# Attention, two MLPs: the second MLP wholly through a seven-product form, the second half of the attention moved beside the first MLP

## Chip, cores and metric

One core of one Trainium2 chip runs the whole program in one launch. The metric is the device time of that core in microseconds (us). Engines: PE multiplies matrices (PEld is its weight load), DVE, ACT and POOL do elementwise work, SP issues nearly all the DMAs.

## Reference

All arrays are float32 at the interface. `q`, `k`, `v` are 8 batches x 8 heads x 576 tokens x 64, `p` has 32 packed queries per head.

```python
def sm_attn(qq, kk, vv):
    s = scale * np.matmul(qq, kk.transpose(0, 1, 3, 2))
    s = s - np.max(s, axis=-1, keepdims=True)
    a = np.exp(s)
    a = a / (np.sum(a, axis=-1, keepdims=True) + 1e-09)
    return np.matmul(a, vv)
p_packed = sm_attn(p, k, v)
out = sm_attn(q, p_packed, p_packed)
...
x = out.transpose(0, 2, 1, 3).reshape(4608, 512)
xn = x / rms * rms_g
g = xn @ w_gate                                  # 512 x 1536
x = (g * (1.0 / (1.0 + np.exp(-g))) * (xn @ w_val)) @ w_out
h = x @ w_in                                     # second MLP, 512 x 2048
g = np.maximum(0.01 * h, h)
return g @ w_out                                 # 2048 x 512
```

The weights come as float64; the kernel turns them into float32 on the chip.

## The kernel before, in words

**Precision.** A value that matters is split into a high and a low part (ACT copies it to a reduced form, DVE or POOL subtracts: `split`, `sub`, L160 to L166), and `mm3` (L135) multiplies with three products: high by high, low by high, high by low. Some products run instead on plain float32 operands; the trace shows each of those as two matrix instructions.

**Attention.** A unit is one batch and four heads, so 16 units. `soft1` (L252) makes the packed keys and values of a unit, `soft2` (L419) the second attention and the sums of squares. Each of their operations has a place in tables (`ONE`, `TWO`), counted in slots; `slot()` (L1009) runs what is due. From unit `FAST` on, the scores are three products of split parts; from unit `FASTQ` on, the squares (`xp`) are. `atf`, which holds a batch's normalised attention, has one buffer.

**First MLP.** Batches go in four pairs; a pair is 24 steps, so 96 steps (L1309). A step multiplies 288 tokens by 256 columns of gate and value weights (24 products of 288 columns: tiles `g`, `v`), and adds the output of the step before to `y_acc` (24 products more: `y`). Four slots pass in a step. In each four steps `fold` (L875) multiplies the attention's packed values into the weights twice (tile `pwps`).

**Second MLP, z stage.** Between the first MLP's step 47 and step 48, tokens 0 to 2047 go through the second MLP in 64 rounds (L1353): 12 products of 512 columns into `zh` (`stage3z`), 12 into `zo` (`stage4z`). Beside them run units 8 to 15 of the attention (`NA = 8`; `LATER`: 22 slots a unit) and half of the 32 conversions of the second MLP's weights (`split_w2`). The other half stands in steps 24 to 39.

**Second MLP, seven products.** At the end tokens 2048 to 4607 go in three pairs of halves (`HALF`, widths 448, 448, 384). A pair needs seven products of sums and differences of the blocks (`ORDER`) where eight plain ones would be needed: 7 x 8 x 6 matrix products into `h` and as many into `o`. Their weights come as pieces of 256 KB through a ring of 10 buffers (`RING = (9, 1)`: 9 in pool `bw0`, which can be filled before the first MLP ends, 1 in pool `bw`). `sums_work` (L1206) makes the sums and differences of weights beside the steps from 48 on.

**Order.** The code is handed to a scheduler, which fixes every engine's instruction order before the run; an engine takes its instructions in that order. SP's queue is one such order: a DMA that waits holds up those behind it.

Of the kernel before, what the change touches and what calls it, by code (L numbers as in the profile page):

```python
# [40 lines left out]
)  # L41
SPLITW = (-68, -58, -57, -57, -8, -6, -1, -1, 9, 10, 13, 13, 21, 29, 29, 29, 37, 37, 45, 42, 50, 53, 59, 61,)
# [4 lines left out]
LATER = (0, 22)  # L47
ZEND = 51
WBUFS = 8
FAST = 8  # L50
FASTQ = 6
# [5 lines left out]
RING = (9, 1)  # L57
GBUFS = 9
CUT = 3
YS0 = 4  # L60
SUM0 = 0
EVERY = (1, 4)
# [4 lines left out]
def pack_attention_moe_kernel(  # L67
# [52 lines left out]
    at_dram = dram.tile([B, P, 2, S], F32, name="at_dram")  # L120
    op_dram = dram.tile([4, 4, P, DM], F32, name="op_dram")
# [3 lines left out]
    cvt = tc.alloc_tile_pool(name="cvt", bufs=1, side="right", reuse_waits="tile")  # L125
    mlpa = tc.alloc_tile_pool(name="mlpa", bufs=1, side="right", reuse_waits="tile")
    mlpb = tc.alloc_tile_pool(name="mlpb", bufs=1, side="right", reuse_waits="tile")
    mlpc = tc.alloc_tile_pool(name="mlpc", bufs=1, side="right", reuse_waits="tile")
    keep = tc.alloc_tile_pool(name="keep", bufs=1, side="left", reuse_waits="tile")
# [54 lines left out]
    g_sb = const.tile([P, KT], F32, name="g_sb")  # L184

# [64 lines left out]
    NA = 8  # L250

    def soft1(i):  # L252
# [4 lines left out]
        def keys():  # L257
# [10 lines left out]
            if i + 1 < NU and i + 1 != NA:  # L268
                last = load_k(*divmod(i + 1, 2))
# [88 lines left out]
        def packed():  # L358
# [21 lines left out]
            if i + 1 < NU and i + 1 != NA:  # L380
                load_v(*divmod(i + 1, 2))
# [33 lines left out]
        if i < NA:  # L415
            return list(zip(ONE[i], parts))
        return [(LATER[0] + LATER[1] * (i - NA) + at, f_) for at, f_ in zip(S1, parts)]

    def soft2(i):  # L419
# [14 lines left out]
        def queries(cs):  # L434
# [6 lines left out]
            if cs[-1] == 1:  # L441
                raw.pop(("q", b, u))
                if i >= FAST:
                    st["qh"] = att.tile([P, NS, 2, T], F32R, tag="raw", bufs=raws, name="qh" + nm)
                    st["ql"] = att.tile([P, NS, 2, T], F32R, tag="tr", bufs=2, name="ql" + nm)
                    split(qT, st["qh"], st["ql"])
                if i + 1 < NU and i + 1 != NA:
                    load_q(*divmod(i + 1, 2))
# [162 lines left out]
        def final(cs, x):  # L611
# [10 lines left out]
            if len(halves) == 2 and 2 * b >= NA:  # L622
                nc.sync.dma_start(out=at_dram[b], in_=atf.pop(b))
# [7 lines left out]
        late = LATER[0] + LATER[1] * (i - NA + 1)  # L631
        for at, f_ in zip(TWO[i] if i < NA else [late + at for at in S2], ops):
            out.append((at, lambda f_=f_: f_(cs)))
# [22 lines left out]
    def load_at(b):  # L656
        if NA <= 2 * b < NU:
            atf[b] = keep.tile([P, 2, S], F32, tag="atf", bufs=1, name=f"atr{b}")
            nc.sync.dma_start(out=atf[b], in_=at_dram[b])

    def split_at(b, cs=(0, 1)):
# [7 lines left out]
        assert 2 * b >= NA or {("at", b, 0), ("at", b, 1)} <= made  # L669
# [4 lines left out]
        if NA <= 2 * b:  # L674
            load_at(b + 1)
# [9 lines left out]
    def convert(raw64, hl, name, whole=False, lay=None):  # L685
# [5 lines left out]
        def begin():  # L691
            c = st["c"] = (
                hl if whole else cvt.tile([P, n], F32, tag="conv", bufs=2, name="cv" + name)
# [25 lines left out]
        def tail():  # L719
# [116 lines left out]
    NW2A = 16  # L836

    def w2_src(i):
        f4, k4 = i // 8, i % 4
        if i % 8 < 4:  # L840
            return w2_in[k4 * P : k4 * P + P, f4 * 512 : f4 * 512 + 512], w1_dram[f4, :, k4]
        m = 4 * f4 + k4
        return w2_out[m * P : m * P + P, :], w2_dram[f4, :, k4]
# [15 lines left out]
    def split_w2(i):  # L859
        if i < 32:  # L860
            until(lambda: i in w2q)
            t = cvt.tile([P, 1024], F32R, tag="w2", bufs=2, name=f"w2s{i}")
            convert(w2q.pop(i), t, f"w2{i}", lay=by_unit if i % 8 < 4 else by_block)

            def done():
                flush_store()
                stores.append((w2_src(i)[1], t))
                if i + 1 != NW2A:
                    load_w2(i + 1)
# [126 lines left out]
    for si in range(4 * NFG - 8, len(steps)):  # L996
        n1, kt = si // 4 + 1, si % 4
        if kt % 2:
            if n1 >= NFG:
                folds[si] = ((n1, kt // 2),)  # L1000
            splits[si] = (n1 * KT + KT + kt - 1, n1 * KT + KT + kt)
# [15 lines left out]
    w1, w2 = {}, {}  # L1017
    ys = {}


    trickle = []

    def drop(count=1, pin=False):
        for _ in range(min(count, len(trickle))):
            ins = trickle.pop(0)()
            if pin:
                tc.keep_in_program_order(ins)

    def load_part(t, src, k_):
        ks = slice(2 * k_, 2 * k_ + 2)  # L1030
        return nc.sync.dma_start(out=t[:, ks].bitcast(F32), in_=src[:, ks])

    def load_w1sb(pool, f, tag=None):
        tags = dict(tag=tag, bufs=1) if tag else {}
        t = w1[f] = pool.tile([P, 4, 1024], F32R, name=f"w1{f}", **tags)
        trickle.extend(lambda k_=k_: load_part(t, w1_dram[f], k_) for k_ in range(2))

    def load_w2sb(pool, f, tag=None):
        tags = dict(tag=tag, bufs=1) if tag else {}
        t = w2[f] = pool.tile([P, 4, 1024], F32R, name=f"w2{f}", **tags)  # L1040
        trickle.extend(lambda k_=k_: load_part(t, w2_dram[f], k_) for k_ in range(2))

    out_st = out.rearrange("(b t s) d -> b s t d", b=B, t=T)

    def store_rows(n, ob, es):

        at, end = n * (P // T), (n + 1) * (P // T)
        while at < end:
            b, s0 = divmod(at, NS)
            k_ = min(end - at, NS - s0)  # L1050
            p0 = (at - n * (P // T)) * T
            nc.sync.dma_start(
                out=out_st[b, s0 : s0 + k_, :, es],
                in_=ob[p0 : p0 + k_ * T, es],
            )
            at += k_


    NZ = 4
    yz = {}  # L1060

    def load_yz(s_, kt):
        if s_ < 2 * NZ:
            l = zw0.tile([P, 512], F32R, tag="yl", bufs=7, name=f"zyl{s_}{kt}")
            i = s_ % NZ
            nc.sync.dma_start(out=l.bitcast(F32), in_=y_dram[:, kt, i * 512 : i * 512 + 512])
            yz["r", s_, kt] = l

    def split_yz(s_, kt):
        if s_ < 2 * NZ:  # L1070
            l = yz.pop(("r", s_, kt))
            h = zw0.tile([P, 512], F32R, tag="yh", bufs=5, name=f"zyh{s_}{kt}")
            act_copy(h, l.bitcast(F32))
            sub(nc.vector, l, l.bitcast(F32), h)
            yz[s_, kt] = (h, l)

    gz, oz, obz = {}, {}, {}

    def stage3z(s_, m):
        at = m % 4 * 2 * P  # L1080
        ms, ml = slice(at, at + P), slice(at + P, at + 2 * P)
        w = w1[m // 4]
        ps = psA.tile([P, 512], F32, tag="h", bufs=2, name=f"zh{s_}{m}")
        for kt in range(KT):
            mm3(
                ps,
                [((w[:, kt, ms], w[:, kt, ml]), yz[s_, kt])],
                start=kt == 0,
                stop=kt == KT - 1,
            )  # L1090
        gf = zwg.tile([P, 512], F32, tag="gf", bufs=2, name=f"zgf{s_}{m}")
        pace[:] = [nc.scalar.activation(out=gf, in_=ps, func=AF.Prelu, alpha=0.01).ins]
        gh = zwg.tile([P, 512], F32R, tag="gh", bufs=3, name=f"zgh{s_}{m}")
        gl = zwg.tile([P, 512], F32R, tag="gl", bufs=3, name=f"zgl{s_}{m}")
        act_copy(gh, gf)
        sub(nc.vector, gl, gf, gh)
        gz[s_, m] = (gh, gl)

    def stage4z(s_, m, t):
        half, i = divmod(s_, NZ)  # L1100
        gh, gl = gz[s_, m]
        k_ = m - half * (NF2 // 2)
        if k_ == 0:
            oz[t] = psA.tile([P, 512], F32, tag=f"o{t}", bufs=1, name=f"zo{s_}{t}")
            if s_:
                obz[t] = zw1.tile([P, DM], F32, tag="ob", bufs=4, name=f"zob{s_}{t}")
            if half:
                nc.sync.dma_start(out=obz[t], in_=op_dram[i, t])
        ts = slice(t * P, t * P + P)
        mm3(  # L1110
            oz[t],
            [((gh[:, ts], gl[:, ts]), (w2[m // 4][:, m % 4, :512], w2[m // 4][:, m % 4, 512:]))],
            start=k_ == 0,
            stop=k_ == NF2 // 2 - 1,
        )
        if k_ == NF2 // 2 - 1:
            ob = obz[t].rearrange("p (a m j) -> p a m j", a=4, m=4)
            o = oz[t].rearrange("p (m a j) -> p a m j", m=4, a=4)
            if half:
                nc.vector.tensor_tensor(out=ob, in0=ob, in1=o, op=ALU.add)  # L1120
                store_rows(i * 4 + t, obz[t], slice(0, DM))
            else:
                act_copy(ob, o)
                nc.sync.dma_start(out=op_dram[i, t], in_=obz[t])

    HALF = ((2048, 448), (2944, 448), (3840, 384))
    WMAX = 448
# [62 lines left out]

    sq_ = {}

    def sums_load(u):
        if u < 4:
# [489 lines left out]
```

## Time and profile before

| | us |
|---|---|
| median of 3 runs (lowest, highest) | 1644.97 (1644.33, 1647.36) |
| the profiled execution: its time | 1646.48 |
| the profiled execution: its span, first to last instruction | 1644.7 |
| busy in that span: PE, PEld, DVE, ACT, POOL | 1582.8, 1405.6, 1028.8, 725.5, 562.1 |

The span is what the rows below divide up; it is 0.3 under the median of the runs. Times in rows are microseconds from the span's start unless marked ns.

### The profile page before, as it was taken

What the parts mean: (1) busy time and instruction counts of PE and PEld (TensorE: products, weight loads), DVE (VectorE), ACT (ScalarE), POOL (GpSimd) and SP (SyncE); (2) the same over time, 40 slices, a digit from 0 to 9 for tenths busy, and PEclk for the clock granted to TensorE, in tenths of its full rate; (3) what the DMA queues carried; (4) which work ended last, traced back from release to release, by engine and by line L of the source; (5) the groups of instructions that cost most, each with busy time, mean ns of one, the idle gap of its engine ahead of it and who ended that gap; (6) DMA issues with size and microseconds to landing.
All of it is one profiled execution on the core that took longest, in us unless ns stands there. A gap on an engine that the chain in (4) does not pass through costs nothing.

```text
span 1644.7 us, 27726 instructions
## 1 busy us (share of the span) xinstructions
PE 1582.8 (96%) x10410; PEld 1405.6 (85%) x10410; DVE 1028.8 (63%) x1778; ACT 725.5 (44%) x1332; POOL 562.1 (34%) x402
## 2 busy tenths in 40 slices
PE   5889999999999999999999799999999999999998
PEld 4568889889898888888877799998999999999998
DVE  7788886767556776555632366644544585496475
ACT  3465555443335655444433433462323553463453
POOL 1234344533222242212221655652225511730530
PEclk8899999999999999999999999999999999999999
DMA  8655452568457645633324956782107778877986
GB/s 273 222 170 171 144 181 78 214 210 283 154 204 240 198 157 187 235 122 88 99 73 165 344 192 234 277 311 90 40 32 248 213 213 253 258 213 216 296 253 195
DMA packets 170902, 318.51 MB, mean 194 GB/s; under 512 B 18192, under 2 KB 82704, under 8 KB 167696
## 3 DMA queue, kind: packets, MB, share of 16 engines
q1 hardware_dynamic: 169136, 315.95, 58.6%
q8 instruction: 83, 1.36, 0.3%
q10 hardware_dynamic: 1632, 0.79, 0.2%
q14 instruction: 51, 0.42, 0.1%
HBM read 245.11 MB, written 71.57 MB: 193 GB/s over the span
## 4 chain that ended last, share of the span: by engine, by line
PE 85%; DVE 6%; DMA 6%; issue 1%; ACT 1%; SPq 1%; POOL 0%; DVEq 0%; ACTq 0%; POOLq 0%
PE y L141 16%; PE h L141 12%; PE o L141 12%; PE zh L141 10%; PE zo L141 10%; PE g L141 8%; PE v L141 8%; PE pwps L894 3%; PE s L141 2%; DMA wo<-in_moe_w_out_dram 1%; PE xp L141 1%; DMA k<-in_k_dram 1%; DMA sl<-w_dram 1%; PE s L469 1%; PE ms L583 1%
## 5 line engine op out<-in xcount | busy, mean ns | idle before, releaser
L141 PE MATMUL y<-hh,wo 128*128 128x288 f32 x1536 | 268.6, 297 | 11.0 <-DVE pw L166 9.7
L166 POOL TENSOR_TENSOR hl<-sg,hh 128x576 fp32r<-128x576 f32 x96 | 146.2, 1523 | 321.7 <-ACT hh L158 319.0
L141 PEld LDWEIGHTS y<-hh,wo 128*128 128x128 f32 x1536 | 225.3, 189 | 19.1 <-DVE pw L166 10.8
L949 DVE TENSOR_TENSOR y_acc<-y_acc,y 128x288 f32<-128x288 f32 x320 | 142.2, 449 | 134.4 <-PE y L141 134.3
L141 PE MATMUL o<-gh,pc 128*128 128x448 f32 (+1 forms) x672 | 184.9, 356 | 0.0
L141 PE MATMUL zo<-w,zgh 128*128 128x512 f32 x512 | 172.3, 392 | 0.0
L141 PE MATMUL y<-hl,wo 128*128 128x288 f32 x768 | 166.2, 296 | 0.0
L141 PE MATMUL zh<-zyh,w 128*128 128x512 f32 x512 | 163.1, 394 | 1.3 <-DVE y_acc L949 1.3
L141 PE MATMUL h<-yh,pc 128*128 128x448 f32 (+1 forms) x672 | 158.5, 357 | 0.5 <-DVE y_acc L949 0.5
L141 PE MATMUL g<-ath,pw 128*128 128x288 f32 x768 | 148.1, 304 | 6.9 <-DVE pw L166 3.5
L141 PEld LDWEIGHTS g<-ath,pw 128*128 128x128 f32 x768 | 115.2, 188 | 40.9 <-ACT hh L158 14.2
L141 PE MATMUL v<-ath,pw 128*128 128x288 f32 x768 | 144.2, 297 | 0.0
L141 PEld LDWEIGHTS h<-yh,pc 128*128 128x128 f32 x672 | 123.8, 188 | 9.0 <-DVE y_acc L949 0.8
L141 PEld LDWEIGHTS o<-gh,pc 128*128 128x128 f32 x672 | 124.6, 188 | 7.2
L158 ACT ACTIVATE hh<-sg 128x576 fp32r<-128x576 f32 x96 | 65.5, 682 | 141.1 <-DVE sg L926 133.3
L141 PEld LDWEIGHTS y<-hl,wo 128*128 128x128 f32 x768 | 124.5, 189 | 3.6 <-issue 2.5
L158 ACT ACTIVATE gh<-g 128x448 fp32r<-128x448 f32 (+1 forms) x168 | 92.5, 560 | 70.4 <-PE o L141 50.2
L166 DVE TENSOR_TENSOR gl<-g,gh 128x448 fp32r<-128x448 f32 (+1 forms) x168 | 105.4, 641 | 28.3 <-ACT gh L158 24.5
L141 PE MATMUL o<-gl,pc 128*128 128x448 f32 (+1 forms) x336 | 119.5, 356 | 0.0
L141 PEld LDWEIGHTS v<-ath,pw 128*128 128x128 f32 x768 | 115.6, 188 | 1.7 <-DVE sn L476 0.8
L141 PEld LDWEIGHTS zh<-zyh,w 128*128 128x128 f32 x512 | 95.3, 188 | 20.8 <-DVE y_acc L949 1.5
L141 PEld LDWEIGHTS zo<-w,zgh 128*128 128x128 f32 x512 | 95.8, 188 | 19.1
(199 smaller groups left out, 3099.4 us busy)
## 6 DMA issues: line engine op xcount, KB each, us to landing
pc<-s_dram SPq DMA_DIRECT2D x192, 256.0 KB
pc<-w_dram SPq DMA_DIRECT2D x144, 256.0 KB
w<-w_dram SPq DMA_DIRECT2D x76, 256.0 KB
wo<-wo_dram SPq DMA_DIRECT2D x36, 512.0 KB
w_dram<-w2s SPq DMA_DIRECT2D x32, 512.0 KB
w<-w_dram SPq DMA_DIRECT2D x16, 1024.0 KB
s_dram<-ss SPq DMA_DIRECT2D x32, 512.0 KB
v<-in_v_dram SPq DMA_DIRECT2D x16, 576.0 KB
```

The lines of the kernel that those rows point to most:

```text
L141: mm = nc.tensor.matmul(ps, lhsT=lh if a == "h" else ll, rhs=rh if b == "h" else rl, start=start and i == 0, stop=stop and i == n - 1,)
L158: nc.scalar.activation(out=o, in_=i, func=AF.Copy, scale=scale)
L166: eng.tensor_tensor(out=o, in0=a, in1=hi.bitcast(F32), op=ALU.subtract)
L469: nc.tensor.matmul(s2[:, k_, :CH], lhsT=PT[:, j].rearrange("p h k -> p (h k)"), rhs=st["qT"][:, c * CS : (c + 1) * CS, j, :], start=j == 0 ...
L583: nc.tensor.matmul(ms[:, k_, :CH], lhsT=ones.bitcast(part.dtype), rhs=part[:, c, :], start=k2 == 0, stop=k2 == len(parts) - 1,)
L894: nc.tensor.matmul(ps[32 * h : 32 * h + 32], lhsT=lpw[2 * (n // NFG) + bb][rs, 2 * u + h // 2, c : c + 32], rhs=w[h // 2][rs], start=True, ...
L949: pace[:] = [nc.vector.tensor_tensor(out=ya, in0=ya, in1=pv, op=ALU.add).ins]
```

## The change

The z stage goes. All 4608 tokens go through the seven-product form, in five pairs of halves of widths 480, 480, 448, 448, 448. Units 8 to 15 of the attention get places in the tables from slot 78 on, 23 slots a unit, so they run beside steps 20 to 72 of the first MLP. `FAST` and `FASTQ` become 16: no unit splits for its scores or squares any more, they are plain float32 products. The second `fold` of four steps stands a step or two earlier (`FK`). The 32 conversions stand at steps 25 to 74, 1.6 steps apart, and each stores its unsplit result too (`c_dram`, 256 KB). The sums of weights start at step 72, read the unsplit weights, all their additions are DVE's, and one item runs in each slot. The ring has 9 buffers, 6 in `bw0`, 3 in `bw`.

```diff
+L0, LP = 78, 23
+ONE += tuple(tuple(L0 + LP * i + at for at in S1) for i in range(8))
+TWO += tuple(tuple(L0 + LP * (i + 1) + at for at in S2[: 10 + 3 * (i % 2)]) for i in range(8))
...
-FAST = 8
-FASTQ = 6
+FAST = 16
+FASTQ = 16
...
-RING = (9, 1)
+RING = (6, 3)
...
-EVERY = (1, 4)
+CONV0, CONV = 25, 1.6
+EVERY = (1, 1)
...
-    NA = 8
+    NA = 16
...
             if not whole:
                 if lay:
+                    nc.sync.dma_start(out=plain, in_=c)
                     hi, lo, c = lay(hl, c)
...
-        if kt % 2:
+        if kt in FK:
...
-    HALF = ((2048, 448), (2944, 448), (3840, 384))
-    WMAX = 448
+    HALF = ((0, 480), (960, 480), (1920, 448), (2816, 448), (3712, 448))
+    WMAX = 480
...
-            src = [w1_dram[f + 2 * a, :, k_ + 2 * b] for a in range(2) for b in range(2)]
+            src = [c_dram[f + 2 * a, k_ + 2 * b] for a in range(2) for b in range(2)]
...
+        def add(o, a, b, op):
+            nc.vector.tensor_tensor(out=view(o), in0=view(a), in1=view(b), op=op)
+
+        todo = [lambda: sums_load(u + 1) if u < 7 else None]
+        for o, a, b, op in ((3, 2, 3, ALU.add), (2, 0, 2, ALU.subtract), (0, 3, 0, ALU.subtract), (1, 1, 0, ALU.subtract)):
+            todo.append(lambda o=o, a=a, b=b, op=op: add(o, a, b, op))
...
+    convs = {}
+    for j in range(32):
+        convs.setdefault(CONV0 + int(j * CONV), []).append(j)
...
-        if n == NFG - 1 and kt == 3:
+        if si == CONV0 - 2:
             load_w2(0)
-        if si == 4 * NFG + 2:
+        if si == 3 * 4 * NFG:
             assert not slots
             att.release()
...
-            za = [(s_, s_ // NZ * 8 + m) for s_ in range(2 * NZ) for m in range(NF2 // 2)]
-            for z, (s_, m) in enumerate(za):
...
-        if 0 <= si - 4 * NFG < NW2A:
-            split_w2(si - 4 * NFG)
+        for j in convs.get(si, ()):
+            split_w2(j)
```

Three places show how the order moves. On PE, the second scores of a late unit (tile `s`) stood before among the z stage's products, as split parts (`qh`, `ql`, `Ph`, `Pl`):

```order
L141 MATMUL zo_5574<-w_5436,zgh_5785 128x512
L141 MATMUL zo_5578<-w_5436,zgh_5785 128x512
L141 MATMUL s_0_5913<-qh_5894,Ph_5726 128x288 x2
L141 MATMUL s_0_5913<-qh_5894,Pl_5727 128x288 x2
L141 MATMUL zo_5578<-w_5436,zgl_5786 128x512
```

Now such scores stand among the first MLP's `v` and `y`, on plain operands:

```order
L143 MATMUL v_6754<-ath_6081,pw_6045 128x288 x4
L143 MATMUL v_6754<-atl_6082,pw_6045 128x288 x2
L470 MATMUL s_0_6762<-qT_6739,PT_6424 128x288 x2
L470 MATMUL s_1_6763<-qT_6739,PT_6424 128x288 x2
L143 MATMUL y_6770<-hh_6576,wo_6063 128x288
L143 MATMUL y_6770<-hh_6576,wo_6186 128x288
```

The unit's products moved from the 512-column products to the 288-column ones, and four logical products of two instructions each replace twelve.

On SP, the queue at the end of the first MLP before (`y_acc` goes out to `y_dram`, `pc` are pieces; nine pieces stand further ahead in the queue):

```order
L830 DMA wo_12826<-wo_dram 128x1024
L830 DMA wo_12911<-wo_dram 128x1024
L952 DMA y_dram<-y_acc_9443 128x576 x4
L952 DMA y_dram<-y_acc_9442 128x576 x4
L1292 DMA pc_13428<-w_dram 128x2x256
L1292 DMA pc_13439<-s_dram 128x512
```

And now, from the last two loads of `wo` on:

```order
L822 DMA wo_10057<-wo_dram 128x1024
L1131 DMA s_dram<-ss_10059 128x2x512
L1131 DMA s_dram<-ss_10088 128x2x512
L1034 DMA yl_10143<-y_dram 128x2x480
L1034 DMA yl_10151<-y_dram 128x2x480
L1034 DMA yl_10153<-y_dram 128x2x480
L1034 DMA yl_10149<-y_dram 128x2x480
L1173 DMA pc_10160<-w_dram 128x2x256
L1173 DMA pc_10598<-s_dram 128x512
L1173 DMA pc_10600<-s_dram 128x512
```

The stores of the weight sums (`s_dram`), the first loads of `y` and the first pieces now come after the last `wo` load, in the last steps; six pieces, where there were nine, stand ahead of the stores of `y_acc`.

On SP around the end of the z stage before (`zob` is an output or partial-output tile, `at_dram` keeps the attention's results, `w` are weights that the next `fold` reads):

```order
L1052 DMA out_dram<-zob_8859 4x32x512
L1108 DMA zob_9213<-op_dram 128x512
L1108 DMA zob_9219<-op_dram 128x512
L1108 DMA zob_9225<-op_dram 128x512
L623 DMA at_dram<-atf_8881 128x1152
L798 DMA w_8925<-w_dram 128x512
```

None of these transfers but the `w` loads exists any more.

## Rows read from the trace of the kernel before

**Rows 1.** Busy time by stretch; columns: stretch, us, PE, PEld, DVE, ACT, POOL, clock, DMA.

```profile
84.90:301.00 216.10, 208.43 (x1675) 182.02 (x1676) 170.49 (x323) 118.19 (x208) 88.79 (x60) 1.00 0.46 148
301.00:479.30 178.30, 171.59 (x1337) 159.31 (x1335) 120.59 (x206) 69.36 (x123) 67.38 (x46) 0.99 0.58 205
479.30:897.90 418.60, 413.22 (x2328) 342.76 (x2329) 239.21 (x385) 199.51 (x367) 99.25 (x67) 1.00 0.50 165
897.90:1244.10 346.20, 336.88 (x2651) 310.72 (x2649) 183.99 (x314) 125.81 (x223) 151.97 (x104) 0.99 0.52 186
1244.10:1637.00 392.90, 392.88 (x2016) 368.99 (x2016) 249.16 (x428) 179.82 (x352) 138.73 (x104) 1.00 0.80 242
1637.00:1644.70 7.70, 0.03 (x1) 0.00 (x0) 1.14 (x2) 0.00 (x0) 0.00 (x0) 0.76 0.52 103
```

**Rows 2.** The chain that ended last, over the span: start us, us, what.

```profile
150.43 1.94 PE s L309 x8
...
228.98 1.82 PE pwps L894 x16
...
523.04 2.72 PE zh L141 x12
...
611.65 1.62 PE s L141 x12
...
1020.18 1.46 PE y L141 x11
1048.02 1.46 PE y L141 x11
...
1244.12 69.45 PE h L141 x336
1313.56 68.63 PE o L141 x336
```

**Rows 3.** PE's groups from 132.3 to 301.0: xcount, busy us, mean ns, idle.

```profile
L469 PE MATMUL s<-qT,PT 128*128 128x288 f32 x32 | 8.5, 406 | 0.0
L309 PE MATMUL s<-kT,pT 128*128 128x288 f32 x24 | 6.7, 410 | 0.1
L558 PE MATMUL xp<-AT,Pm 128*128 128x288 f32 x16 | 5.1, 412 | 0.8 <-ACT sq L565 0.8
L364 PE MATMUL pp<-v,a1T 96*32 96x64 f32 x144 | 2.6, 221 | 0.0
L350 PE MATMUL ta<-ident,e 128*96 128x128 f32 x18 | 2.6, 272 | 0.0
L141 PE MATMUL xp<-ATh,Pmh 128*128 128x288 f32 x8 | 2.4, 296 | 0.0
...
L402 PE MATMUL tp<-ident,Pm 128*128 128x128 f32 x8 | 1.5, 272 | 0.0
L583 PE MATMUL ms<-sqh,ones 128*128 128x288 f32 x4 | 1.1, 294 | 0.0
```

**Rows 4.** Busy time of line 141 (`mm3`) on PE and PEld, the same stretch.

```profile
132.30:301.00 168.70, 136.80 (x947) 127.41 (x946) 1.00 0.45 147
```

**Rows 5.** Timeline of ACT: the first operation after `g`, of steps 24 and 28.

```profile
301.04 0.66 ACT L1446 ACTIVATE sg<-g 128x576 f32<-128x576 f32 x1 [2.08 <-PE g L141]
...
335.45 0.65 ACT L1446 ACTIVATE sg<-g 128x576 f32<-128x576 f32 x1 [2.54 <-PE g L141]
```

**Rows 6.** The chain from 840 to 917: waits at both ends of the z stage's last rounds.

```profile
849.14 9.39 DMA out_dram<-zob
...
859.39 5.98 DMA w<-w_dram
...
902.47 13.69 DMA sl<-w_dram
```

**Rows 7.** Conversions' tile `cvw`, one operation: ns least, median, most; first and last start.

```profile
L715 DVE SCALAR_TENSOR_TENSOR cvw<-w,cvw x32: 646/692/1917, 307.4 to 621.8; 128x512 uint32<-128x512 uint32 x32
```

**Rows 8.** ACT's group of table loads at one line: count, busy us, mean ns.

```profile
L1446 ACT ACT_TABLE_LOAD x9 | 11.5, 1283 | 11.5 <-DVE zob L1120 8.1 <-PE g L141 3.3
```

More of the change, by code (lines that the diff above doesn't have):

```diff
@@ L184, in pack_attention_moe_kernel @@
     g_sb = const.tile([P, KT], F32, name="g_sb")
+    nc.gpsimd.memset(top.tile([P, 120], F32, name="gap"), 0.0)
     qf = q.rearrange("b h (t s) d -> b (h t) (s d)", t=T)
@@ L267, in keys @@
                 split(st["kT"], st["kh"], st["kl"])
-            if i + 1 < NU and i + 1 != NA:
+            if i + 1 < NU:
                 last = load_k(*divmod(i + 1, 2))
@@ L379, in packed @@
             )
-            if i + 1 < NU and i + 1 != NA:
+            if i + 1 < NU:
                 load_v(*divmod(i + 1, 2))
@@ L446, in queries @@
                     split(qT, st["qh"], st["ql"])
-                if i + 1 < NU and i + 1 != NA:
+                if i + 1 < NU:
                     load_q(*divmod(i + 1, 2))
@@ L630, in soft2 @@
         cs = (0, 1)
-        late = LATER[0] + LATER[1] * (i - NA + 1)
-        for at, f_ in zip(TWO[i] if i < NA else [late + at for at in S2], ops):
+        for at, f_ in zip(TWO[i], ops):
             out.append((at, lambda f_=f_: f_(cs)))
@@ L683, in flush_store, with convert @@
             nc.sync.dma_start(out=o, in_=t if t.dtype == F32 else t.bitcast(F32))
-    def convert(raw64, hl, name, whole=False, lay=None):
+    def convert(raw64, hl, name, whole=False, lay=None, plain=None):
         hiw, low = raw64[:, :, 1], raw64[:, :, 0]
@@ L997, in pack_attention_moe_kernel @@
         n1, kt = si // 4 + 1, si % 4
-        if kt % 2:
+        if kt in FK:
+            u_ = FK.index(kt)
             if n1 >= NFG:
-                folds[si] = ((n1, kt // 2),)
-            splits[si] = (n1 * KT + KT + kt - 1, n1 * KT + KT + kt)
+                folds[si] = ((n1, u_),)
+            splits[si] = (n1 * KT + KT + 2 * u_, n1 * KT + KT + 2 * u_ + 1)
         if n1 >= NFG and kt < G:
@@ L1015, in slot @@
                 beside.pop(0)()
[L1017 to L1041, printed above, removed]
-    out_st = out.rearrange("(b t s) d -> b s t d", b=B, t=T)
[L1045 to L1056, printed above, removed]
@@ L1059, in pack_attention_moe_kernel @@
[L1059 to L1075, printed above, removed]
@@ L1077, in pack_attention_moe_kernel @@
[L1077 to L1124, printed above, removed]
@@ L1239, in parts @@
             t = sums.tile([P, 1024], F32R, tag=f"s{x}", bufs=2, name=f"ss{u}{x}")
-            v = t.rearrange("p (f h x) -> p f h x", f=n, h=2)
-            a = raws[k_].rearrange("p (f x) -> p f x", f=n)
-            act_copy(v[:, :, 0], a)
-            sub(nc.vector, v[:, :, 1], a, v[:, :, 0])
+            src = view(k_)
+            if u < 4:
+                v = t.rearrange("p (f h x) -> p h f x", f=n, h=2)
+                pairs = [(v[:, 0], v[:, 1], src)]
+            else:
+                v = t.rearrange("p (n h m a j) -> p n h a m j", n=2, h=2, m=2, a=4)
+                pairs = [
+                    (v[:, y, 0], v[:, y, 1], src[:, y].rearrange("p a (m j) -> p a m j", m=2))
+                    for y in range(2)
+                ]
+            for hi, lo, a in pairs:
+                act_copy(hi, a)
+                sub(nc.vector, lo, a, hi)
             if u < 4:
@@ L1422, in pack_attention_moe_kernel @@
-        if si == 2 * 4 * NFG + SUM0:
             sums = tc.alloc_tile_pool(name="sums", bufs=1, side="left", reuse_waits="tile")
+            beside.append(lambda: sums_load(0))
             held = []
@@ L1428, in pack_attention_moe_kernel @@
                     beside.append(f_)
-                    if k_ % 2 and held:
+                    if k_ and held:
                         beside.append(held.pop(0))
```

211 lines of the change are left out of this document (38 added, 173 removed).

## Prediction

> **What bounds the kernel now.** I first cut the span into stages by the busy time of each stretch [rows 1]. PE is busy for nearly all of every one: 413.2 of 418.6 us in the z stage, 392.88 of 392.90 in the seven-product stage, 208.4 of 216.1 in the first steps of the first MLP. So PE sets the time, and what a change is worth is the work it takes from PE or gives to it, plus the idle time that it makes or fills. Since PE's products overlap, their busy time is not their price; the price is the spacing in the chain that ended last [rows 2]. There twelve 512-column products take 2.72 us (0.2267 each), 336 products of 448 columns take 69.45 us in the `h` half of a pair (0.2067) and 68.63 in the `o` half (0.2043). The same point of two successive groups of four plain steps of the first MLP stands at 1020.18 and 1048.02: 27.84 us for 192 products and two folds. A fold is 16 instructions in 1.82 us. Four plain float32 products take 1.94 us, twelve split ones 1.62.
>
> I make the sum for the span of the profiled execution, 1644.7, and compare with the median, 0.3 higher.
>
> **The change, part by part.**
>
> *Up to step 24.* It ends at 301.0 [rows 5], and the tables of its units stay. Only units 6 and 7 change: their squares were twelve split products each (1.62) and become four plain ones (1.94), 0.6 us more for both. **301.7.** The splits of their operands on ACT and DVE go; I count nothing for that, since PE is the one that is waited for.
>
> *Steps 24 to 95.* Eighteen groups of four at 27.84 are 501.1. The last group has no folds (3.6 less): **497.5**. The last step's `y` products come a step late, 24 at about 0.126: **3.0**. Folds moved a step earlier (`FK`) are the same folds.
>
> *Attention of units 8 to 15.* The first and second scores and the squares are three times 1.94 us a unit [rows 2]. The rest of a unit I take from the stretch with units of the first half [rows 3]: `ta` 2.6 us for 18 instructions, six a unit, 0.87; `pp` 2.6 for 144, 48 a unit, 0.87; `tp` 1.5 for 8, two a unit, 0.38; `ms` 1.1 for 4, with a second group like it, 2.2 for two batches, 0.55 a unit. That makes 5.82 + 2.66 = 8.5 us a unit, **67.8** for eight. As split products they would be 1.0 a unit less. In exchange kl, ql and their kind, splits on ACT and DVE, go; those engines' busy time hides them either way.
>
> *Idle time of PE beside that.* Here the trace has bounds, not a row. Low end: the z stage carried the same eight units and 16 conversions with 5.4 us idle in all, and most of that is at its end (below) [rows 1]. A nearer row: the stretch from 132.3 to 301.0 had five groups of steps with attention at about this density, 168.7 us [rows 4], 29.5 over five plain groups. Of this, 72 plain instructions at 0.2425 are 17.5, the 24 split squares 3.2, `ta`, `pp`, `tp` and `ms` 8.9: 29.6. But line 141 counts 947 products; less the 24 squares that is 923 where five plain groups have 960, so 37 x 0.126 = 4.7 us was idle, 0.9 a group. Thirteen groups (steps 20 to 72) give 12. For the conversions: from 301.0 to 479.3 six plain groups, without the two folds that were put off and with a late `y`, would take 166.4, and the stretch has 178.3: 11.9 us for 16 conversions, 24 for 32. A part of that I take off, since that stretch also split the z stage's first inputs, which is gone: 18. High end: all groups like steps 24 to 28, 34.4 us for 27.84 of plain work [rows 5], 6.6 x 13 = 86. For the sums of weights, whose 32 items of stores stand in SP's queue ahead of some `w` and `wo` loads, I estimate 3: the stretch from 897.9 has 12.8 over twelve plain groups, and the wait at its start (below) takes most. I choose the rows nearest in kind: **33**, with ends 5 and 86.
>
> DVE does not forbid it on the mean. Even if it kept all of the z stage's 239 us of work, it would have 120.6 + 239.2 + 184.0 = 544 us in those 72 steps [rows 1], which take about 600. It keeps far less: the z stage's own splits and output sums go. ACT: the program has 46 table loads where it had 18, because Exp now alternates with Silu; 28 x 1.283 us [rows 8] is 36 us, and with 69.4 + 199.5 + 125.8 that is 431 of 600. It lies beside PE as long as Silu is a step ahead of `y`.
>
> *What goes with the z stage.* At its end PE waited while SP's queue held the weights of the next fold behind stores of `zob`: 9.39 us, then 5.98 for `w`; after it, 13.69 us for the loads of the weight sums [rows 6]. These transfers or their place go, so their idle time goes too; the sum above starts from plain steps and contains none of it. What is late next is the first MLP's own chain through DVE.
>
> *Seven-product stage.* A pair has 672 products. Three pairs of 448 cost 3 x (69.45 + 68.63) = 414.2. A width of 480 is not in the trace. It lies between 0.2055 (mean at 448) and 0.2267 (512); I take the middle, 0.216: 2 x 672 x 0.216 = 290.4, bounds 276 and 305. Together **704.6**, for 392.9 now; 311.7 more, against 418.6 for the z stage with its attention.
> A rule of the Trainium skill would make this cheaper: "TensorE: Matmul & The Clock Gate", Back-to-back issue gap, puts warm products N/2.4 + 2.5 ns apart, which is 202.5 ns for 480, and the two wide pairs at 272, 18 less than mine. The rule gives 189 ns for 448, where the rows have 205, so the trace disagrees for these widths and I go by the rows.
>
> *Tail.* From the last product to the end **7.7** [rows 1], the same stores with one block of columns more.
>
> Sum: 301.7 + 497.5 + 3.0 + 67.8 + 33 + 704.6 + 7.7 = 1615.3; with the 0.3 to the median, **1615.6 us**, 29 less than now.
>
> **The rivals.**
>
> *The first MLP becomes the slow place (slower).* Attention, conversions and the first MLP's own work all meet on DVE and POOL, in fixed order, and PE's queue holds `y` behind scores whose operands are late. The group from 301.0 on had conversions at one a step and lost 6.6 us; there one and the same DVE operation of a conversion takes from 692 ns (median) to 1917 [rows 7]. If each of the 13 groups lost that, idle time is 86 and the time 1669. It decides from (29 + 33) / 13 = 4.8 us a group. Against it: from 132.3 to 301.0 DVE was at 79% (170.5 of 216.1 from 84.9), with dense conversions of the first weights, and PE lost 0.9 a group. "SBUF — State Buffer", Who interferes with whom, in the Trainium skill says that a DVE instruction with two inputs in SBUF and a POOL instruction that reads SBUF block each other for a whole instruction; the 1917 beside 692 agrees. Chance of slower 0.11, and 0.05 that it takes just the gain.
>
> *The attention costs no idle time*, as in the z stage. Then 33 becomes 5, and the time 1587. For it: DVE has fewer splits to do than in any earlier stretch. Against it: 0.9 a group in the nearest stretch. Chance 0.14.
>
> *Pieces come late.* Six pieces lie ready at the start of the last stage where there were nine; they last 36 x 0.216 = 7.8 us instead of 11. Eight stores of 295 KB (2.4 MB) stand between, which at the stage's 242 GB/s [rows 1] take 9.7 us. A wait of up to 4 us at the start, and with one buffer fewer perhaps 2 at each of the four changes of pair: up to 12, so 1628. Against it: a piece lasts 1.30 us at width 480, longer than any now, and the `h` half of the first pair ran without gap. Chance 0.08.
>
> *Wide products cost per column what the 288 ones do*: (27.84 - 3.64) / 192 = 0.126 us, 0.4376 ns a column, so 0.210 at 480 and 8 us less: 1607. By the skill's rule above it would be 1597. The 448 rows speak against it; chance 0.04.
>
> **The numbers.** Forecast 0.58, with its own range 1597 to 1635 (idle time 18 to 50, width 480 up or down 10 in part). Faster is that, the idle-free case, late pieces and cheap columns: 0.84. Same (within 0.2%, about what a measurement can tell, 1641.7 to 1648.3) 0.05, slower 0.11. The range is 1590 to 1645: under it lies about 0.08 (idle-free with cheap 480), over it about 0.12.
>
> **What would show it.** `zh` and `zo` gone; groups of four steps from 20 to 72 of 34 to 37 us (27.84 + 5.2 attention + 1 to 4), and from 80 to 92 of 28 to 29; the first `h` product near 903; 145 us for each wide pair's 672 products and 138 for the others, without gaps; 7.7 at the end. If the groups take 39 or more, the first rival holds. If `h` starts near 903 and the time is still over 1630, the width or the pieces were mis-sized.

## The result and the profile after

The changed kernel takes 1630.48 us (median of 4 runs, 1629.45 to 1632.42), beside 1646.16 for the kernel before in the same session: a ratio of 0.9896, 95% interval 0.9874 to 0.9919. That is 15.7 us less; the forecast was 1615.6, 29 less. The time lies in the range and on the forecast side, and about half of the expected gain is missing.

Busy time by stretch in the changed kernel, cut where the prediction cuts it (steps 4 to 24 come after the first 85 us; then steps 24 to 72, which carry the attention of batches 4 to 7; then the rest of the first MLP; the seven products; the tail). The columns are those of [rows 1].

```profile
85.00:302.20 217.20, 207.98 (x1646) 179.63 (x1646) 174.36 (x323) 121.16 (x210) 90.19 (x63) 1.00 0.52 163
302.20:739.80 437.60, 424.98 (x3367) 367.53 (x3366) 292.06 (x535) 216.68 (x375) 187.10 (x133) 1.00 0.55 182
739.80:913.70 173.90, 170.40 (x1337) 157.67 (x1335) 130.72 (x238) 77.12 (x152) 58.15 (x35) 1.00 0.71 246
913.70:1620.90 707.20, 705.31 (x3360) 630.55 (x3360) 447.37 (x724) 320.13 (x596) 257.13 (x176) 1.00 0.77 230
1620.90:1629.50 8.60, 0.01 (x1) 0.00 (x0) 1.27 (x2) 0.00 (x0) 0.00 (x0) 0.67 0.48 107
```

Step 24 starts at 302.2 (predicted 301.7), the first `h` product at 913.7 (903.0), the stage of the seven products takes 707.2 (704.6) and the tail 8.6 (7.7). So 10.2 of the 14.2 us that the span is over the sum were lost between step 24 and the first `h`. The chain that ended last shows the new stage, where [rows 2] had `zh` and `zo` and two rows of 336 products:

```profile
913.68 73.31 PE h L143 x336
987.00 73.27 PE o L143 x336
1060.26 13.07 PE h L143 x60
1074.67 7.48 DMA pc<-s_dram
1082.29 52.36 PE h L143 x240
1134.65 73.21 PE o L143 x336
...
1358.48 6.26 DMA pc<-s_dram
...
1483.77 68.57 PE h L143 x336
1552.34 68.58 PE o L143 x336
```

A product of width 480 takes 73.31 / 336 = 0.218 us, one of 448 takes 68.57 / 336 = 0.204, now in the `h` half too. From 1060.26 to the next `o` at 1134.65 are 74.4 us, about 1.1 more than without the late piece; the one at 1358 costs about 1.3. That the chain goes over a DMA for 7 us does not mean that PE stood for 7 us.

Between step 24 and step 72 PE has no product under way for only 437.60 - 424.98 = 12.6 us. What ended those waits, in PE's waits of that stretch:

```profile
PE y L143 <- DVE pw L168: 2.7, 3, 1.0
PE g L143 <- ACT sg L1227: 2.5, 2, 1.4
PE y L143 <- ACT y_acc L160: 2.1, 3, 0.9
PE xp L559 <- ACT sq L566: 1.7, 1, 1.7
PE y L143 <- DVE sn L477: 1.3, 1, 1.3
```

All of these but the Silu (`sg`) are DVE or ACT emptying a PSUM bank of the tag `y`, which has four and serves `y`, both banks of a fold, and the attention.

### The profile page after: what moved, and what is told of

It is laid out like the page before. It is cut to its first block, busy times and chain, and to the rows that moved or that the text cites. A ratio compares the mean times of both kernels' runs of the same rounds, so it can differ in the third digit from the quotient of the medians.

```text
span 1629.5 us, 28076 instructions
## 1 busy us (share of the span) xinstructions
PE 1567.1 (96%) x10114; PEld 1377.2 (85%) x10114; DVE 1110.4 (68%) x1942; ACT 767.8 (47%) x1392; POOL 608.6 (37%) x427
## 4 chain that ended last, share of the span: by engine, by line
PE 71%; DVE 12%; DMA 10%; ACT 3%; issue 2%; POOL 2%; SPq 1%; ACTq 0%; DVEq 0%; POOLq 0%
PE o L143 22%; PE h L143 20%; PE y L143 12%; PE v L143 5%; PE g L143 5%; DMA w<-in_moe_w_in_dram 2%; PE pwps L884 2%; DVE y_acc L939 2%; DMA sl<-c_dram 1%; DMA w<-in_moe_w_out_dram 1%; PE s L470 1%; PE xp L559 1%; DMA wo<-in_moe_w_out_dram 1%; DVE pw L168 1%; PE s L312 1%
## 5 line engine op out<-in xcount | busy, mean ns | idle before, releaser
L143 PE MATMUL o<-gh,pc 128*128 128x448 f32 (+1 forms) x1120 | 325.0, 372 | 0.0
L143 PE MATMUL h<-yh,pc 128*128 128x448 f32 (+1 forms) x1120 | 280.2, 372 | 2.4 <-DMA pc<-w_dram 1.0
L143 PEld LDWEIGHTS h<-yh,pc 128*128 128x128 f32 x1120 | 209.7, 188 | 28.4 <-issue 3.9
L143 PEld LDWEIGHTS o<-gh,pc 128*128 128x128 f32 x1120 | 210.4, 188 | 24.2
L168 DVE TENSOR_TENSOR gl<-g,gh 128x448 fp32r<-128x448 f32 (+1 forms) x280 | 179.6, 659 | 49.9 <-ACT gh L160 43.7
L143 PE MATMUL o<-gl,pc 128*128 128x448 f32 (+1 forms) x560 | 207.6, 372 | 0.0
L143 PE MATMUL h<-yl,pc 128*128 128x448 f32 (+1 forms) x560 | 162.8, 372 | 0.0
L1281 POOL TENSOR_TENSOR g<-g,g 128x448 f32<-128x448 f32 (+1 forms) x80 | 115.5, 1444 | 25.3 <-ACT gh L160 13.2
L143 PEld LDWEIGHTS o<-gl,pc 128*128 128x128 f32 x560 | 105.2, 188 | 12.2
L143 PEld LDWEIGHTS h<-yl,pc 128*128 128x128 f32 x560 | 105.2, 188 | 12.2
```

The lines of the kernel that those rows point to most:

```text
L143: mm = nc.tensor.matmul(ps, lhsT=lh if a == "h" else ll, rhs=rh if b == "h" else rl, start=start and i == 0, stop=stop and i == n - 1,)
L168: eng.tensor_tensor(out=o, in0=a, in1=hi.bitcast(F32), op=ALU.subtract)
L1281: eng.tensor_tensor(out=o, in0=a, in1=b, op=ALU.subtract)
```

## The experiments

Where only a span is given below, the kernel ran once; the changed kernel's own spans are 1629.5 and, run again, 1629.4. The first four experiments were chosen from three theories. A: the blocks of the second MLP's weights land late and hold ACT's queue. ACT's waits from 302.2 to 771 spoke for it:

```profile
ACT cvw L686 <- DMA w<-in_moe_w_in_dram: 38.2, 13, 7.4
...
ACT cvw L686 <- DMA w<-in_moe_w_out_dram: 28.2, 12, 4.3
```

B: the conversions' DVE work, slow beside POOL, is what the first MLP waits for. C: the attention's own work on PE and the chains behind it cost more than was counted.

**Blocks loaded two ahead** (`prefetch2`).

```diff
+            load_w2(1)
...
-                load_w2(i + 1)
+                load_w2(i + 2)
```

> Each conversion's float64 block is loaded two conversions ahead instead of one; nothing else changes. In the changed kernel ACT stands 66 us (38.2 + 28.2, 25 waits between 302 and 771) at the head of its queue for these blocks, and PE is idle about 46 us in steps 24 to 95, where the forecast had 33. Theory A (late blocks hold up ACT, and with it Silu, the copies of y and the exponentials): ACT's wait falls under 20 us and the time falls by 15 to 30 us, to 1600 to 1615. Theory B (the conversions' DVE operations are slow beside POOL, whenever their blocks come) and theory C (the attention's own chains): the wait falls, the time stays within 5 us of 1630.

Measured: 1630.66 (4 runs), ratio to the kernel before 0.9888 [0.9858, 0.9918], no change. But ACT's two waits stand at 36.0 and 29.8 us, as before the edit. The trace has the same instructions in the same order as the changed kernel on every engine, and SP issues the blocks when it did (the first three behind step 24 at 331, 334 and 343 us, where it was 330, 332 and 342). The edit had no effect, so this run is one more of the changed kernel and does not part A from the others.

**No conversions** (`no_conv`).

```diff
-            convert(w2q.pop(i), t, f"w2{i}", lay=by_unit if i < 16 else by_block, plain=w2_src(i)[2])
+            nc.sync.dma_start(out=w2_src(i)[2], in_=t[:, :512])
+            nc.sync.dma_start(out=w2_src(i)[1], in_=t)
```

> Leaves out the 32 conversions of the second MLP's weights (their loads and their work on ACT, DVE and POOL); a constant tile is stored in their place, so the stores, the sums of weights and all of PE's work stay. Theories A and B: most of the 38 us of idle time in steps 24 to 71 goes, the span falls by 25 to 38 us to 1592 to 1605. Theory C: it falls by under 10.

Measured: span 1625.5, 4.0 less than the changed kernel. Its window of steps 24 to 72:

```profile
304.40:732.70 428.30, 423.46 (x3367) 368.39 (x3366) 213.82 (x419) 189.38 (x317) 145.56 (x104) 1.00 0.38 125
```

78 us of DVE work are gone from steps 24 to 72, and the stretch is 9.3 shorter, of which most comes back before and behind it: the first `h` starts at 909.2, 4.5 earlier. PE's idle time there falls from 12.6 to 4.8. A and B are not the main cause: the conversions are worth about 4 us of the 18 that they were priced at, by a single run whose order on PE differs from the changed kernel's.

**No attention of batches 4 to 7** (`no_attn`).

```diff
-    fill_slots(range(NA))
+    fill_slots(range(8))
...
-        ah, al = ath[2 * (n // NFG) + bb]
+        ah, al = ath[min(2 * (n // NFG), 2) + bb]
```

> Leaves out the attention of batches 4 to 7; the first MLP takes batches 2 and 3 in their place, so its own work on PE stays. PE's attention work of 67.8 us goes in any case. Theories A and B: the span falls by that and at most 10 more, to 1552 to 1562, and groups of four steps from 24 to 71 still take 2 to 3 us over 27.84. Theory C: it falls by 95 to 105, to 1525 to 1535, and the groups take about 28.

The edit also leaves out the loads of these batches and the splits of their results. Measured: span 1530.3, 99.2 less; C's forecast. The windows:

```profile
303.40:638.90 335.50, 335.50 (x2694) 310.78 (x2693) 222.45 (x378) 132.02 (x236) 119.04 (x82) 1.00 0.62 210
638.90:813.30 174.40, 170.39 (x1336) 157.66 (x1334) 131.88 (x236) 76.13 (x150) 51.61 (x31) 1.00 0.68 233
```

Steps 24 to 72 take 335.5 with all the conversions in them and no idle PE, where twelve plain groups of 27.84 are 334.1. So the plain price was right, the conversions cost PE 1.4 us when no attention stands beside them, and the attention costs 437.6 - 335.5 = 102.1 us there. The last stretch does not change.

**Units 8 to 15 from split parts** (`split_attn`).

```diff
-FAST = 16
-FASTQ = 16
+FAST = 8
+FASTQ = 8
```

> Units 8 to 15 make their scores and squares from split parts again, three products for four (only this part of the change undone). By PE's price alone, 0.96 us a unit, 8 us less. Theory B expects the opposite, since the splits are about 5 us of DVE and 4 of ACT a unit: 0 to 25 us more. Theories A and C: within 8 us below the changed kernel.

Measured: span 1637.1, 7.6 more.

```profile
310.60:747.20 436.60, 419.32 (x3392) 370.49 (x3391) 329.94 (x573) 238.08 (x411) 194.80 (x133) 0.99 0.55 184
```

B's forecast (0 to 25 more) came true here, that of A and C (up to 8 less) did not. PE is busy 5.7 us less from 24 to 72 and idle 4.7 more; DVE has 38 us more to do. Step 24 comes 8.4 us later; about 3 of these, and of the 5.7, are 19 `y` and 48 `pp` products that stand before step 24 here and behind it in the changed kernel. What the split products save on PE is given back as waits. "Plain costs 1 us a unit more" was a price of PE alone.

**Where the attention's 102 us lie.** I took the trace's products by the distance from one start to the next. From 24 to 72 the attention's own products take 52.8 us, 2.3 of them idle time; the first product after a group of plain float32 ones takes 0.35 to the next start where others take 0.13, 41 times, 8.8 (in the chain this tail is in the group: `s` x8 at 1.94). Without the idle time that is 59.3.

Two kernels compared between the same steps do not quite do the same work there. The 48 steps from 24 to 72 make 1152 `y` products, but some of the steps before are still owed at step 24: the windows of the instructions on `y` alone hold 1185 on PE in the changed kernel (first row) and 1154 in `no_attn`. The 31 more are 4.1 us.

```profile
302.20:739.80 437.60, 185.28 (x1185) 164.69 (x1186) 70.88 (x164) 12.43 (x32) 1.00 0.55 182
```

```profile
303.40:638.90 335.50, 183.14 (x1154) 162.80 (x1155) 70.08 (x159) 12.06 (x32) 1.00 0.62 210
```

To the first `h` the two kernels differ by 913.7 - 813.3 = 100.4 us, a sum that no such boundary touches.

Another 15.6 are in the folds: 384 instructions stand 106 ns apart where they stand 66 apart without attention. PE's timeline shows why; first one fold in `no_attn`, then one in the changed kernel:

```profile
307.79 1.09 PE L885 MATMUL pwps<-w,lpw 64*32 64x512 f32 x16
```

```profile
314.52 1.06 PE L884 MATMUL pwps<-w,lpw 64*32 64x512 f32 x8
315.52 0.40 PE L143 MATMUL v<-ath,pw 128*128 128x288 f32 x1
315.85 1.06 PE L884 MATMUL pwps<-w,lpw 64*32 64x512 f32 x8
316.84 0.40 PE L143 MATMUL v<-atl,pw 128*128 128x288 f32 x1
```

Eight instructions into one bank take as long as sixteen into two: in a run most start 7 ns after the one before and overlap. Beside the attention 16 of 24 folds are cut into runs (fold instructions with no other product between them), all but one into two, a bank each, and pay twice. A change between a fold's run and other products costs too: the product before a run takes 0.22 us to the next start and the first one behind it 0.24, where others take 0.13; 41 runs in place of 24 make 3.2 us. With the 12.6 of idle time that leaves 102.1 - 59.3 - 4.1 - 15.6 - 3.2 - 12.6 = 7.3 in other breaks between products, 2.4 of it at the first product behind `ta`, `pp`, `tp` or `ms`.

This gave theory D (the cut folds cost 13 to 16 us that can be had back) and theory E (the four shared banks are what is late; whatever is won on PE comes back as a wait for a bank).

**Folds pinned to alternate** (`pin_fold`).

```diff
+                if done and n > 5:
+                    tc.keep_in_program_order(mm)
+                done += 1
```

> Only the order on PE changes: the products of a fold of both batches stand alternately in its two banks again, as they do in the plain steps, each pinned behind the one before it. In the changed kernel the 384 fold products of steps 24 to 72 stand 106 ns apart (40.9 us), where without the attention they stand 66 ns apart (25.3 us). Theory D (a fold whose two banks are taken one after the other runs its 64-row products singly, about 1.0 us a bank): 13 to 16 us less, the time near 1616. Theory E (there the banks are what is late; a fold that starts only when both are free gives the time back as waits): within 4 us of 1630.5.

Measured: 1635.56 (4 runs), ratio to before 0.9919 [0.9902, 0.9935]: no gain, and over the ranges of both theories. The chain shows that the edit missed its aim: the first product was left free, and goes alone.

```profile
316.07 0.97 PE pwps L885 x2
317.65 1.01 PE pwps L885 x14
...
354.17 1.02 PE pwps L885 x16
```

Two instructions alone cost nearly as much as the other fourteen, and as a whole fold (1.02). Each of the 41 runs of the changed kernel too takes 0.97 to 1.02 us, whatever its length. So D was not yet tested.

**Widths 512, 512, 512, 384, 384** (`w512`).

```diff
-    HALF = ((0, 480), (960, 480), (1920, 448), (2816, 448), (3712, 448))
-    WMAX = 480
+    HALF = ((0, 512), (1024, 512), (2048, 512), (3072, 384), (3840, 384))
+    WMAX = 512
...
-RING = (6, 3)
+RING = (3, 2)
```

> The five pairs have widths 512, 512, 512, 384 and 384 in place of 480, 480, 448, 448 and 448, with as many products; so that it fits, the ring of pieces has 5 buffers in place of 9. Theory F (spacing by the rows: 0.2267 us at 512, 0.1738 at 384): 3 x 672 x 0.2267 + 2 x 672 x 0.1738 = 690.6 for the stage, where 707.2 was measured: 16.6 us less, the time near 1614. Rival G (five pieces last 5 x 6 x 0.2267 = 6.8 us, and each change of pair or half makes one late): the gain is eaten, 1622 to 1632, with waits for pieces in the chain.

Measured: 1662.16 (4 runs), ratio to before 1.0086 [1.0071, 1.0101]; the stage takes 741.0, not 690.6. Rows of its chain, of the first, the fourth and the last pair:

```profile
994.61 73.80 PE o L143 x320
...
1444.87 18.06 PE h L143 x102
1462.94 4.24 DMA pc<-w_dram
1467.22 17.02 PE o L143 x96
1484.26 4.44 DMA pc<-s_dram
...
1592.23 49.23 PE o L143 x281
```

G, the short ring, is right in kind, and costs more than its 1622 to 1632: at width 384 a piece lasts 6 x 0.175 = 1.05 us, so four others cover 4.2, and the loads in the chain take 4.2 to 4.4. F's price was low too: 512 columns take 73.80 / 320 = 0.231 in this stage, where the z stage had 0.227.

From step 24 to 72 this kernel has the changed kernel's order on PE, and took 432.0 against 437.6. That is the spread of one profile.

**No change of ACT's table** (`one_table`). The changed kernel loads a table 46 times; half of these are for the Silu, in ACT's groups (columns as in [rows 8]):

```profile
L1227 ACT ACT_TABLE_LOAD x23 | 29.5, 1283 | 2.1 <-PE g L143 1.7
```

```diff
-                out=e1, in_=e1, func=AF.Exp, bias=st["nb"], accum_out=st["sm"]
+                out=e1, in_=e1, func=AF.Exp if i < 8 else AF.Square, bias=st["nb"], accum_out=st["sm"]
...
-            nc.scalar.activation(out=sn, in_=sn, func=AF.Exp, scale=SCALE)
+            nc.scalar.activation(out=sn, in_=sn, func=AF.Exp if i < 8 else AF.Square, scale=SCALE)
```

> The Exp of units 8 to 15 is replaced by Square (the softmax of batches 4 to 7 is not computed then), so that ACT does not change its table for them. Theory C as it stands now (what the attention costs beyond its products is PE's own: folds taken bank by bank, the first product after a plain float32 one, single waits for banks): at most 4 us less. Rival H (the table loads make ACT late for Silu and for emptying banks, and PE waits for it): 6 to 12 us less.

Measured: span 1621.2, 8.3 less; the stretch, and the longest of PE's waits in it:

```profile
301.40:730.20 428.80, 423.89 (x3367) 368.45 (x3366) 291.02 (x535) 179.94 (x347) 187.29 (x133) 1.00 0.57 185
```

```profile
PE y L143 <- DVE sn L477: 1.9, 1, 1.9
PE y L143 <- ACT y_acc L160: 1.8, 1, 1.8
```

ACT has 37 us less to do, the wait for Silu is gone, and PE's idle time falls from 12.6 to 4.9. H is right in kind. Its size is 3 to 9 us, since unaltered stretches lie between 432.0 and 437.6 and this is one profile. Without the conversions the idle time fell as far (4.8), so the two gains are not to be added.

**Three shared banks in place of four** (`bank3`).

```diff
-    ybufs, raws = 4, 3
+    ybufs, raws = 3, 3
...
-        ps = psA.tile([P, 512], F32, tag="y", bufs=4, name=f"y{n}{bb}{c}{m}")
+        ps = psA.tile([P, 512], F32, tag="y", bufs=3, name=f"y{n}{bb}{c}{m}")
```

> The tag of PSUM banks that y, the folds and the attention share has three buffers in place of four. Theory E (shared banks that are late to be emptied are what PE waits for beside the attention): steps 24 to 72 take at least 15 us more than the 437.6 of the changed kernel, and the plain steps from 72 on at most 5 more. Theory D with PE's own costs alone: steps 24 to 72 take at most 6 us more than that, since a fold that has its two banks one after the other already runs as it would then.

Measured: span 1693.7. Windows, and the first row of PE's waits from 24 to 72:

```profile
326.50:786.30 459.80, 426.27 (x3327) 370.25 (x3315) 278.32 (x527) 216.74 (x372) 178.44 (x130) 0.98 0.51 171
786.30:976.20 189.90, 183.56 (x1352) 161.35 (x1350) 146.29 (x246) 78.76 (x153) 62.49 (x37) 1.00 0.67 233
```

```profile
PE g L143 <- ACT sg L1227: 17.1, 15, 2.8
```

22 us more beside the attention is E's number, but 16 more in the plain stretch is not (E allowed 5; 27 `y` products more in it, which the stretch before lacks, are 3.6), step 24 comes 24 later, and the wait that grew is for Silu. With three banks the whole order on ACT and PE is another one. Inconclusive for E: banks are short everywhere, not beside the attention alone.

**Folds in one run** (`probe_fold`): a product of two columns takes the first bank, and the fold waits, pinned behind it, until it has the second.

```diff
+            nc.tensor.matmul(
+                outs[0][:32, :2],
+                lhsT=lpw[2 * (n // NFG) + bbs[0]][rs, 2 * u, :32],
+                rhs=w[0][rs, :2],
...
-            for bb, ps in zip(bbs, outs):
+            for bb, ps in list(zip(bbs, outs))[::-1]:
...
+                if n > 5:
+                    tc.keep_in_program_order(mm)
```

> A fold beside the attention is made to run as one uninterrupted run: a two-column product into its first bank takes the bank, and the 16 products wait pinned behind it until the second bank is free too. In the pinned order tried before, a first fold product went alone and took 0.97 us, the other 14 together 1.01: a run of 2, 8, 14 or 16 cost about 1.0 us each. Theory D: 24 folds in runs of 16, 384 products in about 25 us where 40.9 to 43.0 were measured, and less by 10 to 15 us in steps 24 to 72 than the changed kernel run beside it. Theory E: the folds take 25 to 27 us too, but a bank that lies empty meanwhile makes the products around them wait: within 4 us of the changed kernel run beside it.

Beside it ran the changed kernel again (`after_again`).

> The changed kernel unaltered, beside the run before it on the same chip. Its steps 24 to 72 took 437.6 us; a kernel with the same order on every engine up to the last stage (that of the widths of 512) took 432.1 there. Expected: 430 to 438, so that a difference of 6 us in one profile of this stretch shows nothing.

Measured: 1630.97 (4 runs) and 1630.79 (4 runs), ratios to before 0.9904 [0.9888, 0.9921] and 0.9901 [0.9885, 0.9918]. First `probe_fold`, then `after_again`, steps 24 to 72:

```profile
312.80:735.30 422.50, 408.56 (x3343) 364.07 (x3342) 282.36 (x528) 212.16 (x371) 182.21 (x130) 1.00 0.55 186
```

```profile
302.90:737.60 434.70, 424.27 (x3366) 367.39 (x3365) 292.83 (x535) 217.25 (x374) 187.75 (x133) 1.00 0.55 183
```

The 384 fold instructions with their 48 small ones now take 29.9 us, and steps 24 to 72 are 12.2 shorter, by the number as D said. But step 24 comes 9.9 later, and the boundary flatters the stretch: 23 `y` products (1161 here, 1184 in `after_again`) and 48 `pp` stand before it now, about 4 us.

```profile
312.80:735.30 422.50, 179.82 (x1161) 160.21 (x1162) 69.26 (x161) 12.58 (x32) 1.00 0.55 186
```

For the same work the stretch gained about 8 us, less than D's 10, and the first `h` starts at 912.6 beside 912.9. The edit had also turned the banks of the early folds about, so two more kernels left those as they were, or gave them the same run.

**Only the late folds, and all of them** (`probe_late`, `probe_all`).

```diff
-        if n > 5:
+        runs = n > 5
+        if runs:
...
+            for bb, ps in list(zip(bbs, outs))[:: -1 if runs else 1]:
```

> As the fold with the two-column product before it, but the changed order of the two banks too is used only for the folds from step 20 on; in the kernel before this one the reversed banks of the earlier folds had moved the products of the first 24 steps, which then ended at 312.8 us in place of 302.9, and the 12.2 us won in steps 24 to 72 were given back there. Theory D: step 24 at 302 to 305 again, steps 24 to 72 in 420 to 427, the whole near 1620 (ratio to the kernel before 0.984). Theory E (the time comes back in some other place whenever the folds are held for two banks): 1627 to 1633.

> The same for every fold of both batches, the eight of the first 20 steps among them, which stand beside the attention of the first batches. Theory D: about 0.9 us a fold less there, up to 7 us, so 1613 to 1620. Theory E: more than the kernel beside it that leaves the early folds as they were, 1622 to 1635, with step 24 later than 305.

Measured: 1633.85 (5 runs), ratio 0.9908 [0.9890, 0.9925]; and 1635.32 (6 runs), 0.9918 [0.9901, 0.9935]. Neither is faster than the changed kernel. `probe_late`, a fold in PE's timeline, the window of steps 24 to 72, and the longest of PE's waits from 24 to 72:

```profile
318.91 0.22 PE L883 MATMUL pwps<-w,lpw 64*32 64x2 f32 x2
319.06 0.40 PE L143 MATMUL v<-ath,pw 128*128 128x288 f32 x1
319.30 0.43 PE L143 MATMUL v<-atl,pw 128*128 128x288 f32 x2
319.66 1.09 PE L895 MATMUL pwps<-w,lpw 64*32 64x512 f32 x16
```

```profile
306.60:738.90 432.30, 415.40 (x3415) 369.59 (x3414) 286.20 (x536) 214.35 (x373) 183.41 (x131) 1.00 0.56 184
```

```profile
PE y L143 <- DVE pw L168: 4.9, 5, 2.3
PE y L143 <- ACT y_acc L160: 2.7, 3, 1.3
PE pwps L883 <- ACT a1T L160: 1.7, 1, 1.7
PE pwps L895 <- ACT y_acc L160: 1.6, 1, 1.6
```

The fold runs as one, and PE is busy 9 to 10 us less than in the changed kernel. The stretch is only 2 to 5 shorter: idle time went from 12.6 (10.4 in `after_again`) to 16.9, mostly for banks that DVE and ACT have yet to empty, and step 24 is 4 later. E's forecasts of the whole came nearest (held for `probe_fold`, 0.9 and 0.3 us over their ranges in the other two); D's, near 1620 and 1613 to 1620, failed. The waits of `probe_late` show banks; for the time lost before step 24 in `probe_fold` and `probe_all` I have only the changed order, and no run parts the two. "TensorEngine Tiling (Array Packing)" in the Trainium skill says under PSUM Bottleneck that packing speeds up TensorE but not the emptying of PSUM, which can then be the limit; the waits of `probe_late` agree. Under Key Properties it says that a change of tiling mode drains TensorE; the lone `v` product between two runs above, which takes 0.33 us from start to start beside the 0.13 of others, agrees in kind.

## Why the prediction was half right

*Up to step 24*: 302.2 for 301.7. *Plain steps*: `no_attn` has 335.5 for twelve groups, 27.96 each where 27.84 was taken. The last stretch, 72 to `h`, was to take six groups with 3.6 off for the missing folds, 3.0 for the late `y` and 3 for the sums, 169.4; it takes 173.9. A plain fold is 1.02 us, not the 1.82 of [rows 2], so 2.0 should have been taken off; the rest is mostly that stretch's 3.5 us of idle PE.

*Attention of units 8 to 15 and idle time beside it*: here the step failed. 67.8 for products and 12 for waits make 79.8; with and without the attention the kernels differ by 101.6 from step 24 to the first `h`, and by 100.4 from the start. The products came out at 59.3 in steps 24 to 72, and unit 8's first scores, about 2.5 us, stand before. That is 6 under the forecast, since `ta`, `pp`, `tp` and `ms` had been priced by their busy time, which overlaps (18 `ta` of [rows 3] are busy 2.6 us and take 1.6 by their starts). The idle time is 12.6, almost the 12 forecast, although it was worked out from products that ran dearer and not from waits: in the stretch of [rows 4] PE is idle only 168.7 - 167.5 = 1.2 us, where the prediction read 4.7.

What was missing is that the attention makes PE's other work dearer: 15.6 us for folds cut in two, 3.2 for the changes between their runs and other products, and 7.3 in other breaks, of which I did not attribute some 5. The prediction had the sign of it in [rows 2]: a fold of 1.82 us, read from a stretch with attention, was taken for the plain fold. In the trace its sixteen instructions start eight at 228.91 and eight at 229.74, as those of a cut fold do. The plain group stayed right, since 27.84 was measured as a whole, but the product price of 0.126 inside it was too low ((27.84 - 2 x 1.02) / 192 = 0.134), and the loss of folds vanished from the count of [rows 4].

*Conversions*: 18 forecast, 1.4 (without attention) to 4 (with it). The high figure was read from a stretch in which the z stage's first inputs were split too. So two wrong terms of opposite sign, +21.8 for the attention and -11.6 for all else to the first `h`, hid each other in part. That groups of four steps take 36.5 us on the mean of 24 to 72, inside the 34 to 37 foretold, is in part luck: what comes on top of the products is mostly folds and breaks, where idle time and conversions were meant.

*Table loads*: "they lie beside PE as long as Silu is a step ahead" was wrong by 3 to 9 us. These are no further term: the profile without them has 4.9 us of idle time from step 24 to 72 where 12.6 were.

*Seven-product stage*: 0.218 for 0.216 at width 480 is 2.6 us more, 0.204 for 0.2055 at 448 is 2.5 less, which is luck, and late pieces are about 2.4: 707.2 for 704.6. The Trainium skill's rule of N/2.4 + 2.5 ns ("TensorE: Matmul & The Clock Gate", Back-to-back issue gap, where it is the gap of isolated products) gives 0.2025 at 480; the rows disagree, as the prediction held.

*Rivals*: the slow first MLP (1669) did not come: what goes beyond the attention's products is (102.1 - 59.3 - 4.1) / 12 = 3.2 us a group, under the 4.8 from which it decides and the 6.6 of its price. (The 1917 ns that it names are an operation at 554.75, in the z stage; in the group from 301.0 the longest is 1798.) Attention without idle time (1587) did not come either. Late pieces came at a fifth of their price. Cheap wide products did not.

What stays open: where the time before step 24 goes in the kernels with folds in one run, and whether a fifth bank for the shared tag would turn the folds' saving into time. PSUM's eight banks are all in use (two each for `g` and `v`, four for the shared tag), and this was not tried.

## What to carry to other kernels

Work that is moved beside a stage that fills PE costs more than its own products: price it by a stretch that already has both and by leaving it out, not by adding up rows. When a row is used as the price of a repeated step, look where it stands; a fold's row from a crowded stretch was nearly twice that of a plain one. Before two kernels are compared between the same steps, count the products that lie between: 12.2 us of gain were 8. Once an engine's instructions are cut down, ask what empties their results: of the 9 to 10 us that PE saved in `probe_late`, 4 to 6 came back as idle time, mostly in waits for PSUM banks.

## What was not expected of the hardware

A run of products of 64-row, 32-column weights, 512 columns wide, took 0.97 us for two instructions, 0.99 for eight into one bank and 1.02 for sixteen that alternate between two; sixteen that start in two lots of eight, as in [rows 2], took 1.82. Per column, wide products of the last stage are not quite alike: 0.450 ns at 512, 0.455 at 480, 0.456 at 384 and 448. One and the same order of instructions on PE took 432.0 to 437.6 us in four profiles of one stretch (the changed kernel twice, `prefetch2`, `w512`), while the changed kernel's whole runs agreed within 0.2%.
